# Layer norm of the last 1536 tokens in rows of features: normalization of already transposed x on VectorE in place of TensorE's transposition

## The chip, the cores and the metric

The kernel runs on one core of one Trainium2 chip. The metric is the device time of one execution in microseconds (us), the median of several runs; lower is better. The five engines of a core run their own queues of instructions, each in order, and meet only at semaphores: TensorE (PE in the profile; its weight loads are PEld), VectorE (DVE), ScalarE (ACT), GpSimd (POOL) and SyncE (SP), which here only issues DMAs.

## The reference

One transformer block on 2048 tokens of 512 features, all in float32: a layer norm without scale, 32-head attention with heads of 16 features, a gate computed by a two-layer perceptron with squared ReLU, and a residual.

```python
xn = _layernorm(x)                       # mean and variance over the 512 features
qkv = xn @ wqkv                          # 512 -> 3 * 512, split into q, k, v of 32 heads of 16
p = softmax(q @ k.T * 16 ** -0.5)        # 2048 x 2048 for each head
s = concat(p @ v) @ wo
h = relu(xn @ w1 + b1)                   # 512 -> 1792
g = silu((h * h) @ w2 + b2)              # 1792 -> 512
out = x + s * g
```

## The kernel before

A product of float32 matrices is made of three float32r products: each operand is split into a high part (`hi`) and the rest (`lo`), and the sum of hi·hi, hi·lo and lo·hi is accumulated in one bank of PSUM. With 512 features on 4 blocks of 128 partitions (`ko`), a tile of 128 x 512 outputs takes 12 matmuls.

The work has three stages. In the **opening** x is read, normalized, transposed and split into `xTs[c]` (features on partitions, 512 tokens of chunk c, hi and lo), and the first tiles of the projection are made: K, Q of the first 4 feature blocks (`qk_tile(4, c)` is the K tile and `qk_tile(0, c)` the Q tile of chunk c for heads 0 to 7) and V (`v_tile(c, tt)`, 128 tokens). In the **lead** (L1451 on) the other projection tiles run as half matmuls on both halves of TensorE's rows, between the first maxima of scores. In the **main loop** (L1675 on) scores, exponentials, the product with V, the perceptron and the output projection share TensorE.

The order of PE, ACT, DVE and POOL in the opening is written out by hand: each engine executes in the order in which the program emits instructions. SP's order in the opening is not by hand, it is set by the scheduler. The opening loop (L1327) goes over the 16 tiles of 128 tokens with a skew:

- `ln_stats(t)` (L1221): DVE takes the statistics of the tile (`bn_stats`, `bn_aggr`), ACT the square root.
- `ln_norm(t)` (L1229): DVE takes the reciprocal and the shift; for t of 2 and more ACT writes the normalized tile `xn` (L1241).
- `ln_high(t)` (L1244): PE transposes the tile by 4 matmuls with the identity (L1248) into a bank of PSUM, ACT copies it to the hi part (L1250). `ln_low(t)` (L1253): DVE subtracts for the lo part (L1256).
- `pump(n)` (L1264) emits n matmuls of the projection tiles: those of the list `ahead` first (`qk_first()`, that is the K and the Q tile of chunk 0 in halves of 256 tokens; then the K tiles of the later chunks), else those of `rest` (V and Q tiles).

A projection tile takes one of three PSUM banks (`se`, L1050) until `led` holds something. What is done with a finished tile stands in `qk_done` (L1072): with `quick`, ACT copies the hi part and DVE subtracts (`split_psum`, L104); else ACT copies it and POOL does both parts. While `hold[0]` is true, finished tiles wait for the next `let_go()`. Quick is for m of 0 and 4 after `hold[0]` is false, which before is after the loop. `v_done` (L1134) is one copy by ACT.

After the loop the rest of the opening follows: the K tiles left in `ahead`, the loads of the first K and Q heads (`load_k`, L1400, and `load_q`, L1402; both from DRAM, where K and Q were stored), the split of further weights, and the tiles of `rest` up to `v_tile(2, 0)` (L1407 to L1415). Then comes the lead, whose first score maximum needs the K of all 2048 tokens of the first head pair and Q of chunk 0.

`spill(c, k)` (L1308) stores the normalized x of a chunk to DRAM for the perceptron. Before, chunks 0 and 1 are spilled in the opening, 2 and 3 in the lead (`SPILLS`, rounds 5, 9, 13, 17).

Of the kernel before, what the change touches and what calls it, by code (L numbers as in the profile page):

```python
# [9 lines left out]
F32 = mybir.dt.float32  # L10
# [7 lines left out]
P = 128  # L18
S = 2048
D = 512  # L20
# [14 lines left out]
NXR = 16  # L35
EVAC = (1, 6, 7, 9, 11, 14)
# [3 lines left out]
SPILLS = (5, 9, 13, 17)  # L40
# [17 lines left out]
def kernel(  # L58
# [8 lines left out]
    b2: bass.AP,  # L67
    out: bass.AP,
# [12 lines left out]
    sp_d = dram.tile([S, D], F32, name="sp_d")  # L81
    xn_d = dram.tile([2, P, KO, S], F32, name="xn_d")
# [32 lines left out]
    with ExitStack() as ph:  # L115
# [42 lines left out]
        def load_k(qd, n):  # L158

            p, j, i = n // 6, n // 3 % 2, n % 3  # L160
            if n % 6 == 0:
                kas[qd, p] = ring("ka")
            h = 4 * qd + 2 * p + j
            nc.sync.dma_start(
                kas[qd, p][64 * j + DH * i : 64 * j + DH * (i + 1), :].bitcast(F32),
                k_d[h // 8][i % 2, (h % 8) * DH : (h % 8 + 1) * DH, :],
            )
# [850 lines left out]
        def qk_terms(m, c, ps):  # L1018
            wq, m0 = wq_cols(m)
            ms = slice(m0, m0 + P)  # L1020
            xT = xTs[c]
            t = terms3(ps, [
                (lambda a, q, ko=ko: wq[q, a, ko, ms], lambda b, q, ko=ko: xT[q, b, ko])
                for ko in range(KO)
            ])
            if m == 4 and c == 0:

                t = [t[k] for k in (0, 3, 6, 9, 2, 5, 1, 4, 7, 10, 8, 11)]
            return t
# [183 lines left out]
        def load_x(t):  # L1213
            xts[t] = xp.tile([P, D], F32, name="xt", bufs=12)
            nc.sync.dma_start(xts[t], xf[t * P : (t + 1) * P, :])

        mvs = {}
        rstds = {}
        pts_ = {}

        def ln_stats(t):  # L1221
            stats = xp.tile([P, 6], F32, name="stats")
            nc.vector.bn_stats(stats, xts[t])
            mvs[t] = xp.tile([P, 2], F32, name="mv", bufs=3)
# [3 lines left out]

        def ln_norm(t):  # L1229
            rstd = rstds.pop(t)  # L1230
            xn = xp.tile([P, D], F32, name="xn", bufs=3)
# [46 lines left out]
        def exp_mm(st, j, pts, spare):  # L1278
# [5 lines left out]
            else:  # L1284
# [10 lines left out]
                if all(t is not x for d in pts_all.values() for x in d.values())  # L1295
# [8 lines left out]
                    mybir.EngineType.Activation, mybir.EngineType.DVE, mybir.EngineType.Pool,  # L1304
                }
# [12 lines left out]
        raw_m = load_w("wm", 2 * P, ((0, P), (D, P)))  # L1318
        for t in range(2, 6):
            load_x(t)  # L1320
        raw_v = load_w("wv", D, ((2 * D, D),))
        for t in range(6, NT):
            load_x(t)
        for vt in vts:
            nc.vector.memset(vt[:, :, DH:], 1.0)
        fill_ring("ka", 0, -1.0)
        for i in range(NT + 3):  # L1327
            if i in (2, 3):

                kos = slice(2 * i - 4, 2 * i - 2)  # L1330
                if i == 2:
                    ln_norm(1)
                    ln_high(0)
                    split_w(wa_t, kos, slice(0, 2 * P), raw_m[:, kos])
                    ln_low(0)
                else:
                    ln_high(1)
                    split_w(wa_t, kos, slice(0, 2 * P), raw_m[:, kos])
                    ln_stats(2)
                    ln_low(1)  # L1340
                    ln_norm(2)
                    ln_stats(3)
            else:
                if i < NT:
                    ln_stats(i)
                if 0 <= i - 1 < NT:
                    ln_norm(i - 1)
                if 2 <= i - 3 < NT:
                    ln_low(i - 3)
                if i == 4:  # L1350

                    pump(10)
                if 0 <= i - 2 < NT:
                    ln_high(i - 2)
            if 5 <= i < 9:
                split_w(wa_t, i - 5, slice(2 * P, 2 * P + D), raw_v[:, i - 5], True)
            let_go()
            if 9 <= i < 11:
                fill_ring("ka", 1, -1.0, (32 + 64 * (i - 9),))
            if i in (11, 12):  # L1360
                fill_ring("qm", i - 11, 0.0)
            if i == 11:
                raw_r = [load_w("wv", 3 * P, ((P, 3 * P),))]
            if i in (13, 14):
                spill(0, i - 13)
            if i in (16, 18):
                spill(1, (i - 16) // 2)
            if i >= 4:
                pump({4: 6, 7: 14, 8: 12}.get(i, 8 if i < 7 else 7 if i < 11 else 6))
            if i == 3:  # L1370
                ahead.append(qk_first())
            if i >= 7 and (i - 3) % 4 == 3:
                c = (i - 3) // 4
                ahead.append(qk_tile(4, c))
                rest.append(qk_tile(0, c))
                order.append(("qk", 0, c))
            if i >= 3 and (i - 3) % 4 == 3:
                c = (i - 3) // 4
                rest += [v_tile(c, tt) for tt in range(4)]
                order += [("v", c, tt) for tt in range(4)]  # L1380
# [19 lines left out]
        for n in range(12):  # L1400
            load_k(0, n)
# [5 lines left out]
        pump(47)  # L1407
# [16 lines left out]
        lead.enter_context(tc.manual_schedule(engines={mybir.EngineType.SP}))  # L1424
# [10 lines left out]
        def lead_rounds():  # L1435
            for i in side_rounds(specs, single):
                if i % 6 == 0:
                    now[0] = i // 6
                    run_waiting()
                    if i // 6 in SPILLS:  # L1440
                        c, k = divmod(SPILLS.index(i // 6), 2)
                        spill(c + 2, k)
# [266 lines left out]
_INS = ['A_x', 'A_wqkv', 'A_wo', 'B_w1', 'B_b1', 'B_w2', 'B_b2']  # L1709
# [23 lines left out]
```

## Time and profile before

| what | value |
|---|---|
| time, median of 3 runs | 1621.21 us (1621.0 to 1621.35) |
| the profiled execution: time | 1621.38 us |
| the profiled execution: span of the core | 1619.6 us |
| TensorE busy | 1607.3 us, 99% of the span |
| VectorE busy | 1352.4 us, 84% |
| ScalarE busy | 1187.2 us, 73% |
| GpSimd busy | 534.1 us, 33% |

The profile is that of one execution, so its durations add up to that execution's own time of 1621.38 us, 1.8 us of which lie around the span. Busy shares are means over the whole span; the change touches the opening alone, which the views by window show.

### The profile page before, as it was taken

Reading aid. Unit: us, or ns where it says so; the run is one execution under the profiler, and the core shown is the slowest. Engines: PE = TensorE matmul, PEld = TensorE weight load, DVE = VectorE, ACT = ScalarE, POOL = GpSimd, SP = SyncE. Lnnn points to the kernel's source line nnn. Section 1 sums busy time; section 2 is a strip of 40 time slices with the busy share of each in tenths; the row PEclk is TensorE's granted clock in tenths of the full one; section 3 lists DMA queues with packets and bytes.
Section 4 is the critical chain, followed back from the end, with each engine's and each line's share of the span. In section 5 each row is a group of like instructions: output and inputs, shape, how many; then the busy total and the mean of one; then the engine's idle time right before and its main releaser. Section 6 shows DMA issues by size and latency. Waiting matters only on the chain.

```text
span 1619.6 us, 36065 instructions
## 1 busy us (share of the span) xinstructions
PE 1607.3 (99%) x13660; PEld 939.7 (58%) x13660; DVE 1352.4 (84%) x2307; ACT 1187.2 (73%) x2347; POOL 534.1 (33%) x610
## 2 busy tenths in 40 slices
PE   8999999999999999999999999999999999999998
PEld 7799665556545654664466446645654565445543
DVE  7486888888888888888888888888888888887754
ACT  7212777777777777877777777777777777778886
POOL 6436667133113311331133113311331123214621
PEclk9999999999999999999999999999999999999999
DMA  8967556434333333423333334323432252237655
GB/s 290 244 237 234 174 156 160 132 96 128 81 104 94 106 88 88 131 87 101 90 107 100 91 89 118 115 71 90 131 107 73 65 163 76 64 102 228 207 177 169
DMA packets 164173, 209.19 MB, mean 129 GB/s; under 512 B 59136, under 2 KB 79360, under 8 KB 162432
## 3 DMA queue, kind: packets, MB, share of 16 engines
q1 hardware_dynamic: 163856, 206.63, 43.9%
q8 instruction: 108, 1.77, 0.5%
q14 instruction: 65, 0.53, 0.1%
q10 hardware_dynamic: 144, 0.26, 0.0%
HBM read 148.90 MB, written 56.34 MB: 127 GB/s over the span
## 4 chain that ended last, share of the span: by engine, by line
PE 99%; DVE 1%; DMA 0%; issue 0%; ACT 0%; DVEq 0%
PE po L406 31%; PE pd_t L258 19%; PE pm_t L320 17%; PE se L1286 15%; PE pd_t L226 5%; PE pm_t L1157 4%; PE pm_t L226 1%; PE pd_t L1157 1%; PE se L1127 1%; PE se L1061 1%; PE se L320 1%; PE pm_t L1248 0%; PE pd_t L1127 0%; DVE mx L327 0%; PE po L1061 0%; DMA xt<-in_A_x_dram 0%
## 5 line engine op out<-in xcount | busy, mean ns | idle before, releaser
L327 DVE TENSOR_REDUCE mx<-pm_t 128x1 f32<-128x512 f32 x1910 | 1188.3, 684 | 174.5 <-PE pm_t L320 84.8
L1298 ACT ACTIVATE pt<-se 128x512 f32<-128x512 f32 x1894 | 975.4, 613 | 234.3 <-PE se L1286 187.0
L320 PE MATMUL pm_t<-ka,qm 64*128 64x512 f32 x1910 | 761.0, 419 | 0.0
L1286 PE MATMUL se<-qe,ka 64*128 64x512 f32 x2005 | 677.3, 396 | 0.0
L406 PE MATMUL po<-pt,v 128*32 128x512 f32 x3820 | 520.8, 605 | 0.2 <-DVE tsm L849 0.2
L320 PEld LDWEIGHTS pm_t<-ka,qm 64*128 64x128 f32 x1910 | 335.2, 184 | 236.0 <-DVE mx L327 224.5
L1286 PEld LDWEIGHTS se<-qe,ka 64*128 64x128 f32 x2005 | 338.9, 184 | 19.8 <-ACT xr L1298 1.7
L258 PEld LDWEIGHTS pd_t<-xc,w1s 64*128 64x128 f32 x2352 | 292.1, 187 | 82.2 <-issue 82.2
L258 PE MATMUL pd_t<-xc,w1s 64*128 64x256 f32 x2352 | 332.3, 288 | 0.0
L258 PE MATMUL pd_t<-w2t,hT 64*128 64x512 f32 x1080 | 300.1, 410 | 0.0
L258 PEld LDWEIGHTS pd_t<-w2t,hT 64*128 64x128 f32 x1080 | 179.3, 184 | 82.4 <-issue 75.5
L571 POOL TENSOR_TENSOR r<-r 128x512 f32<-128x512 f32 x56 | 58.2, 1040 | 353.5 <-ACT r L568 353.5
L406 PEld LDWEIGHTS po<-pt,v 128*32 128x32 f32 x3820 | 76.7, 108 | 147.1 <-issue 125.6
L327 DVE TENSOR_REDUCE mx<-se 128x1 f32<-128x512 f32 x121 | 77.9, 686 | 26.1 <-PE pm_t L1157 17.3
L590 POOL TENSOR_TENSOR u<-u,b_t 128x512 f32<-128x512 f32 x16 | 20.6, 1285 | 209.1 <-ACT u L589 209.1
L568 ACT ACTIVATE r<-pd_t,b_t 128x256 f32<-128x256 f32 x112 | 46.9, 470 | 57.1 <-PE pd_t L258 55.0
L99 POOL TENSOR_SCALAR sh<-tr 128x32 fp32r<-128x32 f32 x30 | 6.5, 217 | 213.6 <-DVE tr L371 213.6
L1157 PE MATMUL pm_t<-xT,wr_t 64*128 64x512 f32 x408 | 74.0, 388 | 0.0
L100 POOL TENSOR_TENSOR hT<-r,hT 128x512 fp32r<-128x512 f32 x56 | 72.2, 1290 | 4.7
L226 PE MATMUL pd_t<-w2t,hT 64*128 64x512 f32 x264 | 68.7, 392 | 0.0
L1157 PEld LDWEIGHTS pm_t<-xT,wr_t 64*128 64x128 f32 x408 | 60.7, 185 | 0.0
L455 POOL TENSOR_TENSOR ot<-ot,hl 128x512 f32<-128x512 f32 x27 | 34.7, 1285 | 65.4 <-DMA hl<-r_d 51.7
(177 smaller groups left out, 1398.9 us busy)
## 6 DMA issues: line engine op xcount, KB each, us to landing
w1s<-w_d SPq DMA_DIRECT2D x196, 256.0 KB
qm<-q_d SPq DMA_DIRECT2D x384, 32.0 KB
ka<-k_d SPq DMA_DIRECT2D x96, 128.0 KB
qe<-q_d SPq DMA_DIRECT2D x384, 32.0 KB
q_d<-hl SPq DMA_DIRECT2D x16, 512.0 KB
g<-g_d SPq DMA_DIRECT2D x32, 256.0 KB
k_d<-hl SPq DMA_DIRECT2D x15, 512.0 KB
on_d<-hl SPq DMA_DIRECT2D x116, 64.0 KB
```

The costliest lines, as they stand in the source:

```text
L100: (lo or nc.gpsimd).tensor_tensor(dst[1], raw, dst[0].bitcast(F32), op=ALU.subtract)
L226: mm = nc.tensor.matmul(out_, lh(r), rh(r), start=first_ and lane == 0, stop=last_ and lane == 1, skip_group_check=True,)
L258: mm = nc.tensor.matmul(out_, lh(r), rh(r), start=first_ and lane == 0, stop=last_ and lane == 1, skip_group_check=True,)
L320: nc.tensor.matmul(ps, qms[u][p][64 * j : 64 * j + 64, qb * P : (qb + 1) * P], kas[qd, p][64 * j : 64 * j + 64, kc * 512 : (kc + 1) * 512] ...
L327: return nc.vector.tensor_reduce(mxs[u][:, c, kc : kc + 1], ps, axis=AX.X, op=ALU.max)
L406: nc.tensor.matmul(po[32 * j : 32 * j + 32, :], vs[qd][:, (4 * kb + j) * VW : (4 * kb + j) * VW + 32], pts[j], start=(kb == 0), stop=(kb = ...
L455: nc.gpsimd.tensor_tensor(ot, ot, rb, op=ALU.mult)
L568: nc.scalar.activation(r[:, i], ps[:, i * CW : (i + 1) * CW], AF.Relu, bias=b1_t[:, fo : fo + 1])
L571: nc.gpsimd.tensor_tensor(r, r, r, op=ALU.mult)
L1157: mm = nc.tensor.matmul(out_, lh(r), rh(r), start=first_ and lane == first, stop=last_ and lane != first, skip_group_check=True,)
L1286: nc.tensor.matmul(se, kas[qd, j // 2][b : b + 64, kb * P : (kb + 1) * P], qes[u][j // 2][b : b + 64, :], start=True, stop=True,)
L1298: return nc.scalar.activation(pts[j], se, AF.Exp, scale=0.25)
```

## The change

The host hands over two more arrays: `x_t`, x with features in rows (for each chunk and each half of 256 tokens, 128 partitions by 4 blocks by 256 tokens), and `w_m`, the first K and Q weight columns in the layout of the tile that they are loaded to. Tokens 0 to 511 (chunk 0) are normalized and transposed as before. For chunks 1 to 3:

- the statistics of a tile still come from x with tokens in rows, and `bn_aggr` puts mean and variance into columns of a tile `lns[c]` of the chunk;
- `ln_rows(c)`: ACT takes the square root of the 4 variances at once, DVE the reciprocal and a transposition in blocks of 32, and SP writes 4 small pieces to DRAM as rows of 512 means and 512 factors;
- `ln_back(c)`: SP reads these rows back into all 128 partitions (512 KB);
- `ln_half(c, h)`: DVE subtracts the row of means from the half chunk and multiplies by the row of factors, two blocks at a time, in place; ACT copies the hi part, POOL subtracts for the lo part.

So the 48 transpositions of these tiles on TensorE, with their banks, the 12 hi copies by ACT from PSUM, the 12 lo subtractions by DVE and the 12 normalizations by ACT are gone. The loop of the opening is written out anew, with its pumps: the order of the matmuls after chunk 0 is now K of chunk 1, Q of chunk 1, K of chunk 2, K of chunk 3, V of chunk 1, Q of chunk 2, first V of chunk 2. `hold[0]` is false before the first K and Q tiles are done, so all of these are quick. The hi part of the V weights is made by ACT in place of POOL. `load_k` is issued in two parts of 1024 tokens. Chunk 1 is spilled in the lead, where `SPILLS` has two more rounds. SP's order is by hand in the opening as well. The buffers of x tiles go from 12 to 7, those of `xn` from 3 to 2.

```diff
-SPILLS = (5, 9, 13, 17)
+SPILLS = (5, 9, 13, 17, 21, 25)
...
+            elif m == 4:
+                t = [t[k] for k in (0, 3, 6, 9, 2, 5, 8, 11, 1, 4, 7, 10)]
...
         def ln_stats(t):
             stats = xp.tile([P, 6], F32, name="stats")
             nc.vector.bn_stats(stats, xts[t])
+            if t >= 4:
+                c, n = divmod(t, 4)
+                nc.vector.bn_aggr(lns[c][:, :8].rearrange("p (k t) -> p t k", k=2)[:, n], stats)
+                return
...
+        def ln_rows(c):
+            m = lns[c]
+            nc.scalar.activation(m[:, 4:8], m[:, 4:8], AF.Sqrt, bias=eps_t)
+            nc.vector.reciprocal(m[:, 4:8], m[:, 4:8])
+            tr = xp.tile([P, 32], F32, name="lnt")
+            nc.vector.transpose(tr, m)
+            for q in range(4):
+                nc.sync.dma_start(
+                    ln_d[c].rearrange("k t n -> (k t) n")[:, 32 * q : 32 * q + 32],
+                    tr[32 * q : 32 * q + 8],
+                )
+
+        def ln_back(c):
+            row = lnrs[c] = xp.tile([P, 2, 512], F32, name="lnr")
+            nc.sync.dma_start(
+                row.rearrange("p k n -> p (k n)"),
+                ln_d[c].rearrange("k t n -> (k t n)")[None, :].to_broadcast([P, 1024]),
+            )
+
+        def ln_half(c, h):
+            ns = slice(256 * h, 256 * h + 256)
+            row, raw, xT = lnrs[c], xrs.pop((c, h)), xTs[c]
+            pairs = (slice(0, 2), slice(2, 4))
+            for kos in pairs:
+                for k, op in ((0, ALU.subtract), (1, ALU.mult)):
+                    nc.vector.tensor_tensor(
+                        raw[:, kos], raw[:, kos], row[:, k : k + 1, ns].to_broadcast([P, 2, 256]), op=op
+                    )
+                nc.scalar.activation(xT[:, 0, kos, ns], raw[:, kos], AF.Copy)
+            for kos in pairs:
+                nc.gpsimd.tensor_tensor(
+                    xT[:, 1, kos, ns], raw[:, kos], xT[:, 0, kos, ns].bitcast(F32), op=ALU.subtract
+                )
+
+        def load_xt(c, h):
+            raw = xrs[c, h] = xp.tile([P, KO, 256], F32, name="xr_", bufs=3)
+            nc.sync.dma_start(raw, x_t[c, h])
...
+            else:
+                ln_low(3)
+                for ko in (2, 3):
+                    split_w(wa_t, ko, slice(2 * P, 2 * P + D), raw_v[:, ko])
+                for t in range(4, 8):
+                    ln_stats(t)
+                    if t == 4:
+                        load_x(11)
+                ln_rows(1)
+                ln_back(1)
+                for t in (12, 13, 14):
+                    load_x(t)
+                load_xt(2, 0)
+                ln_stats(8)
+                load_x(15)
+                hold[0] = False
+        def add_chunk(c):
+            if c:
+                ahead.append(qk_tile(4, c))
+                (ahead if c == 1 else rest).append(qk_tile(0, c))
+                order.append(("qk", 0, c))
+            rest.extend(v_tile(c, tt) for tt in range(4))
+            order.extend(("v", c, tt) for tt in range(4))
+        add_chunk(0)
+        ln_stats(9)
+        pump(24)
+        for t in (10, 11):
+            ln_stats(t)
+        ln_rows(2)
+        ln_back(2)
+        pump(12)
+        ln_half(1, 0)
+        load_xt(2, 1)
+        pump(6)
+        for t in (12, 13):
+            ln_stats(t)
+        ln_half(1, 1)
+        load_xt(3, 0)
...
+        pump(6)
+        for t in (14, 15):
+            ln_stats(t)
+        ln_rows(3)
+        ln_back(3)
+        pump(12)
+        ln_half(2, 0)
+        load_xt(3, 1)
+        pump(12)
+        add_chunk(1)
+        pump(6)
+        ln_half(2, 1)
...
+        pump(6)
+        ln_half(3, 0)
+        pump(12)
+        for n in range(12):
+            load_k(0, n, slice(0, 1024))
+        add_chunk(2)
+        ln_half(3, 1)
+        raw_r = [load_w("wv", 3 * P, ((P, 3 * P),))]
+        pump(12)
+        add_chunk(3)
+        pump(12)
+        for k in range(2):
+            spill(0, k)
...
         for n in range(12):
-            load_k(0, n)
+            load_k(0, n, slice(1024, S))
         qms[0] = load_q(0, "qm")
...
-        pump(47)
```

More of the change, by code (lines that the diff above doesn't have):

```diff
@@ L35 @@
 NXR = 16
+NXT = 7
 EVAC = (1, 6, 7, 9, 11, 14)
@@ L1218 @@
         rstds = {}
+        lnrs = {}
+        xrs = {}
+        lns = {c: xp.tile([P, 32], F32, name=f"lns{c}", bufs=1) for c in range(1, 4)}
+        for m in lns.values():
+            nc.vector.memset(m, 1.0)
         pts_ = {}
```

125 lines of the change are left out of this document (63 added, 62 removed).

## The prediction, made before the changed kernel ran

> **What bounds the kernel now.** I read the page's first part, then the busy times by window of the first 60 us, then the chain of work that ended last in that stretch, then DVE's, POOL's and SP's timelines beside it.
>
> ```profile
> PE 1607.3 (99%) x13660; PEld 939.7 (58%) x13660; DVE 1352.4 (84%) x2307; ACT 1187.2 (73%) x2347; POOL 534.1 (33%) x610
> ```
>
> TensorE is the bound of the whole, so a microsecond by which the opening is longer or shorter should stand in the total. The change is confined to the opening.
>
> ```profile
> core 0: us, PE busy (x) PEld busy (x) DVE busy (x) ACT busy (x) POOL busy (x), PEclk, DMA share, GB/s
> 0.00:10.00 10.00, 2.92 (x12) 2.41 (x13) 5.82 (x25) 4.29 (x8) 5.68 (x10) 1.00 0.82 275
> 10.00:20.00 10.00, 10.00 (x68) 9.96 (x68) 9.33 (x30) 8.57 (x17) 8.16 (x9) 1.00 0.82 303
> 20.00:30.00 10.00, 10.00 (x54) 8.23 (x53) 8.09 (x26) 8.71 (x19) 8.31 (x8) 1.00 0.68 196
> 50.00:60.00 10.00, 10.00 (x45) 8.04 (x44) 0.00 (x0) 1.80 (x3) 7.33 (x10) 1.00 0.83 116
> ```
>
> PE is full from 10 us on. DVE is nearly as full as PE until 30 us (9.33, then 8.09 of 10) and has nothing to do at 50 to 60. So the question is not what PE saves, but whether DVE, which receives the work, can deliver in time.
>
> ```profile
> 9.02 2.60 PE se L1061 x10
> ...
> 15.72 0.44 PE pm_t L1248 x4
> ...
> 17.55 1.67 PE se L1061 x14
> ...
> 19.89 2.32 PE se L1127 x10
> ...
> 37.32 0.44 PE pm_t L1248 x4
> 37.75 2.79 PE se L1127 x12
> ...
> 60.13 2.80 PE pd_t L1127 x12
> ```
>
> The chain is PE without a gap. From 15.72 to 37.32 it holds 12 groups of 4 transpositions at 0.44 us: tiles 4 to 15, those that the change removes. A projection tile is 12 matmuls in 2.80 us (0.233 each). The last one ends at 60.13 + 2.80 = 62.93: there the lead begins. I work out this moment for the changed kernel.
>
> **What is removed.** On PE, 12 x 0.44 = 5.3 us, all on the path. On ACT 12 normalizations and 12 copies, on DVE 12 subtractions and 12 pairs of small operations, all hidden before. With PE alone the lead would begin at 57.6.
>
> **What is added, DVE first.** Its in-order queue goes on from `ln_low(3)`:
>
> ```profile
> 15.39 0.68 DVE L1256 TENSOR_TENSOR xT<-pm_t,xT 128x512 fp32r<-128x512 f32 x1
> 15.98 0.68 DVE L1223 BATCH_NORM_STATS2 stats<-xt 128x6 f32<-128x512 f32 x1
> 16.70 0.18 DVE L1225 BATCH_NORM_AGGREGATE mv<-stats 128x2 f32<-128x6 f32 x1
> 16.80 0.13 DVE L1232 RECIPROCAL rstd<-rstd 128x1 f32<-128x1 f32 x1
> ```
>
> From start to start a 128x512 operation takes about 0.60 us (15.39 to 15.98) if the next does not need it, else its full 0.68; statistics of one tile take 0.72 + 0.10 = 0.82. After the change `ln_low(3)` still waits for PE and ACT; I put its end at 15.5, up to 0.5 earlier than before since fewer statistics stand ahead of it.
>
> ```profile
> L371 DVE STREAM_TRANSPOSE tr<-m 128x32 f32<-128x32 f32 x32 | 6.5, 202 | 0.1
> L1227 ACT ACTIVATE rstd<-mv,eps_t 128x1 f32<-128x1 f32 x16 | 4.7, 294 | 4.0 <-DVE mv L1225 2.4 <-DVE rstd L1232 1.4
> L106 DVE TENSOR_TENSOR hl<-se,hl 128x512 fp32r<-128x512 f32 x2 | 1.4, 692 | 7.0 <-ACT hl L105 7.0
> L100 POOL TENSOR_TENSOR hl<-raw,hl 128x512 fp32r<-128x512 f32 x5 | 6.5, 1292 | 0.4
> L815 DVE TENSOR_TENSOR g<-g,s 128x512 f32<-128x512 f32 x12 | 8.8, 741 | 0.3
> L380 SPq DMA_DIRECT2D sh_d<-sh x32: 319/320/432, 118.9 to 1554.3; - x32
> L441 SPq DMA_DIRECT2D hl<-r_d x27: 540/552/594, 240.2 to 1419.6; - x27
> 0.74 2.75 DMA xt<-in_A_x_dram
> ```
>
> 1. Statistics of tiles 4 to 7: 4 x 0.82 = 3.3, to 18.9. Square root 0.29, reciprocal 0.15, transposition 0.20, with hand-overs: 19.7.
> 2. The rows go through DRAM. Four small writes, issued at 0.34 each by SP, the last at 20.8. A write's landing is not in the trace; the first x tile took 2.75 from issue, of which its 256 KB at the 380 GB/s of full queues are 0.7, so I take 2.1 to 2.2 for a small one: 23.0. The broadcast of 512 KB (issue 0.55, then 3.0) lands at 26.6. SP waits there, and the loads of x tiles 12 to 15 behind it land by about 30, before they are needed.
> 3. Meanwhile DVE does the statistics of 8 to 11 (3.3), the quick subtractions of the first K and Q tiles (1.3) and the second chunk's rows (0.8): free at 25.1. The rows are the later: `ln_half(1, 0)` begins at 26.6. Landings of 1.0 less each would give 25.1; of 4.1 (K's last store, before, 47.48 to 51.61) about 30.
> 4. The six halves are 24 operations of 128x512 with both operands in SBUF. Their nearest row is L815 (two SBUF operands; least 0.65). That one operand is a broadcast row has no price in the trace at 512; I take none. With a mean of 0.62 for dependent and independent ones, 14.9 us.
>
> **The price that I think decides** is that these 24 meet POOL's 12 subtractions of 1.29 us, which read SBUF at the same time.
>
> ```profile
> 1564.13 0.69 DVE L813 TENSOR_TENSOR g<-pd_t,g 128x512 f32<-128x512 f32 x1 [0.33 <-PE pm_t L1286]
> 1564.38 0.73 POOL L100 TENSOR_TENSOR hl<-ot,hl 128x256 fp32r<-128x256 f32 x1
> 1583.99 1.82 DVE L815 TENSOR_TENSOR g<-g,s 128x512 f32<-128x512 f32 x2
> 1584.07 1.20 POOL L100 TENSOR_TENSOR hl<-tot,hl 128x256 fp32r<-128x256 f32 x1
> ```
>
> At 1564 DVE reads one operand from PSUM: POOL's subtraction takes its plain 0.73. At 1584 DVE has two operations with both operands in SBUF, and everything stretches: POOL's takes 1.20 instead of 0.73, the two of DVE 1.82 instead of some 1.25. 1.25 + 0.73 is 1.98, near the whole stretch of 1583.99 to 1585.81: they ran one after the other. The Trainium skill (SBUF — State Buffer, section Who interferes with whom) says that a VectorE instruction with two SBUF inputs and a GpSimd instruction that reads SBUF exclude each other for their whole length. The trace agrees with it.
>
> So from 26.6 on one port carries the 24 operations (14.9) and, ahead of the last of them, 10 of the 12 subtractions (12.9): 54.4. Statistics of tiles 12 to 15 and two quick subtractions lie beside POOL's. Moments in which neither uses the port (the third chunk's square root; the quick subtraction that stands behind ACT's copies) I put at 1.4: DVE ends `ln_half(3, 1)` at 55.8.
>
> **PE.** The first K and Q tiles end at 19.89 less three transposition groups: 18.6. Four V tiles take 11.2, and 0.7 is lost since the second needs the bank of the first K tile, which DVE frees at about 22.0: chunk 0 is used up at 30.5. Then K of chunk 1 needs both halves of chunk 1, by the same working at 34.6, and the bank of a V tile whose copy stands on ACT behind the hi copies: 35.8. K of chunk 3, in this order only two tiles after Q of chunk 1, is the last to wait: 55.8, 0.65 for ACT's copy, 10 matmuls of 0.233, 0.3 for the last lo part: 59.1. Six tiles follow without a wait: 59.1 + 6 x 2.80 = 75.9. That is 13.0 us later than 62.93.
>
> **Two smaller prices.** PE is idle for 5 to 7 us twice. At the start, after its first idle time, 10 matmuls of 256 columns took 2.60 us (0.26 each), later 14 took 1.67 (0.12), while the granted clock reads 1.00. From 9.02 to 15.72 the chain holds 24 of them in 5.0 us. At 0.12 they would be 2.9. So a restart may cost 0 to 2.1, with the transpositions between them up to 3.0. The Trainium skill (TensorE: Matmul & The Clock Gate, Part 1: The HAM clock gate) halves the clock after an idle window of some 3.4 us for about as long; by it the last restart would cost an estimated 1.7.
>
> SP's queue now runs in the written order: it holds the second halves of the K loads and then Q until K of chunk 3 is stored, and all of them behind the bias loads.
>
> ```profile
> 25.18 3.59 SPq L1397 DMA_DIRECT2D b_t<-in_B_b_dram  x1
> ...
> 47.48 0.38 SPq L1016 DMA_DIRECT2D k_d<-hl  x1
> ...
> 51.61 6.42 SPq L164 DMA_DIRECT2D ka<-k_d  x12
> 58.80 4.61 SPq L153 DMA_DIRECT2D qm<-q_d  x5
> ```
>
> K of chunk 3 is ready to be stored at 61, lands at about 64; biases (up to 4) keep SP until 64 to 68; 12 loads take 6.4 and six of Q 3.0 and a landing of 2: Q is there at 76 to 79.5. Against 75.9 that is 0 to 3.5. The two overlap: a PE that restarts slowly waits less for Q. I take 2.0 for both together. The extra 4.5 MB (rows of x_t and broadcasts) ride in the DMA queues beside the wait for DVE. The spill of chunk 1 moves into the lead, where I cost it at nothing; it would matter if it held back K or Q loads, which come earlier in the same queue.
>
> **Sum.** 13.0 + 2.0 = 15.0 on 1621.4 of the profiled execution: 1636.4; its median stands 0.2 lower: **1636.2**.
>
> **Rivals.**
> - *DVE alone sets the pace, port free* (0.18). If POOL and DVE can run beside each other here, DVE's own queue is left: 26.6 + 14.9 + statistics 3.3 + rows 0.8 + quick subtractions 1.2 + waits for ACT and for dependent results 4.1 = 50.9. Lead at 70.8: +7.9, 1629.2, up to 1631 with a slow restart. For it: only one place of the trace shows the collision at 512 elements. Against: that place is clean.
> - *No change* (0.09). If also the waits vanish (rows land early, ACT never late), DVE has 15.5 + 12 x 0.82 + 3 x 0.35 + 24 x 0.60 + 4 x 0.60 = 43.2, the lead begins at about 63, and the time is 1621 to 1624.5. This is the floor of my own prices, which is why I hold a gain to be unlikely.
> - *PE keeps the pace, faster* (0.05). The one mechanism: the halves are ready before PE asks, at 30.5, 36 and 39, and the 5.3 us are kept: 1616. It decides at the end of `ln_half(3, 1)`: under 39.9 the gain exceeds 3.2 us. From the floor of 43.2 that asks for less than 0.47 per operation of 512 elements; no DVE row with two operands of that size is under 0.65.
> - *K and Q loads still later* (0.06): landings of 4 us in each of the round trips, two of them in line, add 4 and more to the forecast: 1641 to 1647.
>
> **Chances and range.** Forecast 0.62, with a range of its own of 1632 to 1642. The range of 8 in 10 reaches down over the free port and up over some of the late loads: 1627 to 1643. A measurement of this kernel can tell about 0.2%, 3.2 us, from no change. Faster by more 0.05, within 0.09, slower 0.86.
>
> **What would show it.** In the windows of the changed kernel PE's count falls from 45 per 10 us to under 30 between 30 and 57, and DVE is busy at 40 to 55, where it was idle. The chain should run over the subtract and multiply of `ln_half` and the first lead matmul start at 73 to 80. If port sharing is right, the group of these operations has a mean near 0.9 us and POOL's subtraction shows over 1.4; if wrong, 0.7 and 1.29, with the lead at 71. If chunk 1's broadcast lands after 28, step 2 is short. I am wrong altogether if PE stays full from 10 to 60 us.

## The result, and the profile after

| | before | changed |
|---|---|---|
| time, median | 1621.11 us (1620.78 to 1621.35, 4 runs) | 1644.69 us (1644.6 to 1646.86, 4 runs) |
| profiled execution: time | 1621.38 us | 1644.64 us |
| profiled execution: span | 1619.6 us | 1642.8 us |

The ratio is 1.0149, with a 95% interval of 1.0131 to 1.0166: slower by 1.5%, clear of noise. The forecast was 1636.2 us with a range of 1627 to 1643. The direction was right; the time lies 1.7 us above the range. Between the profiled executions the loss is 1644.64 - 1621.38 = 23.3 us, where the forecast had 15.0.

The first line is the busy time of each engine over the whole span, and the fence below it the windows of 10 us from 30 to 90 us:

```profile
PE 1611.2 (98%) x13612; PEld 929.0 (57%) x13612; DVE 1364.9 (83%) x2308; ACT 1179.5 (72%) x2330; POOL 543.0 (33%) x610
```

```profile
core 0: us, PE busy (x) PEld busy (x) DVE busy (x) ACT busy (x) POOL busy (x), PEclk, DMA share, GB/s
30.00:40.00 10.00, 5.40 (x17) 3.98 (x16) 5.88 (x13) 2.55 (x5) 7.89 (x6) 0.83 0.66 215
40.00:50.00 10.00, 5.59 (x17) 3.70 (x16) 8.62 (x10) 3.50 (x6) 6.54 (x6) 0.76 0.74 241
50.00:60.00 10.00, 5.64 (x14) 3.74 (x13) 6.72 (x10) 3.49 (x6) 7.51 (x8) 0.67 0.59 209
60.00:70.00 10.00, 10.00 (x40) 8.10 (x39) 0.69 (x1) 3.33 (x7) 2.40 (x3) 0.89 0.79 269
70.00:80.00 10.00, 10.00 (x45) 7.64 (x44) 0.69 (x1) 2.46 (x5) 9.53 (x14) 1.00 0.83 224
80.00:90.00 10.00, 4.67 (x23) 3.52 (x22) 3.10 (x5) 1.43 (x2) 0.82 (x1) 0.66 0.46 159
```

In the kernel before, the two windows that the prediction doesn't show are these:

```profile
30.00:40.00 10.00, 10.00 (x55) 8.32 (x54) 5.81 (x15) 7.15 (x14) 4.54 (x8) 1.00 1.03 382
40.00:50.00 10.00, 10.00 (x45) 8.04 (x44) 1.38 (x2) 4.04 (x8) 6.37 (x8) 1.00 0.98 336
```

So TensorE executed 45 to 55 matmuls in each 10 us between 30 and 60 us and was full. Now it executes 17, 17 and 14 there. There is a second hole, which the forecast had only as 0 to 3.5 us: 23 matmuls between 80 and 90 (before, 88, of the lead), when the projection tiles are done. The granted clock (PEclk) falls with the holes, to 0.83, 0.76, 0.67 and again 0.66; before, it read 1.00 in every window up to 100 us.

TensorE's timeline says what each hole waits for. Its columns are start, duration, engine, line, operation, tile, shape, count, and in brackets the idle time ahead of the group and what ended it:

```profile
35.23 7.27 PE L1067 MATMUL se<-xT,wa_t 128*128 128x512 f32 x24 [4.60 <-ACT vt L1142]
46.80 5.69 PE L1067 MATMUL se<-xT,wa_t 128*128 128x512 f32 x12 [4.30 <-ACT xT L1272]
56.74 5.82 PE L1067 MATMUL se<-xT,wa_t 128*128 128x512 f32 x12 [4.25 <-ACT xT L1272]
62.40 2.94 PE L1133 MATMUL se<-wa_t,xT 128*128 128x512 f32 x12
...
79.22 0.50 PE L1163 MATMUL pm_t<-wa_t,xT 64*128 64x512 f32 x1
...
85.52 0.76 PE L324 MATMUL se<-ka,qm 64*128 64x512 f32 x1 [5.33 <-DMA qm<-q_d]
```

The three K tiles (chunks 1, 2, 3) each wait over 4 us: the first for a bank that ACT frees by a copy that stands behind its hi copies, the others for the hi copies themselves, and these wait for DVE. The last one is done at 62.40, six tiles follow without a wait, and the lead begins at 79.22. The first matmul of the maxima (L324) then waits 5.33 us for Q, until 85.52. Before, these two moments were:

```profile
62.86 0.50 PE L1157 MATMUL pm_t<-wa_t,xT 64*128 64x512 f32 x1
...
63.44 0.39 PE L320 MATMUL se<-ka,qm 64*128 64x512 f32 x1
```

So of the 23.3 us, 79.22 - 62.86 = 16.4 arise until the lead begins and (85.52 - 79.22) - (63.44 - 62.86) = 5.7 from there to the first maxima. The remaining 1.2 follow at once: the rows of the maxima from 85.52 on take 0.62 to 0.79 us where they took 0.39 before. From the first rows of the maxima on the two traces run alike.

DVE's timeline is where the first 16.4 come from:

```profile
26.30 2.75 DVE L1269 TENSOR_TENSOR xr__237<-xr__237,lnr 128x512 f32<-128x512 f32 x4 [1.35 <-DMA lnr<-ln_d]
...
30.58 3.46 DVE L1269 TENSOR_TENSOR xr__239<-xr__239,lnr 128x512 f32<-128x512 f32 x4
...
39.99 2.75 DVE L1269 TENSOR_TENSOR xr__394<-xr__394,lnr 128x512 f32<-128x512 f32 x4 [3.55 <-DMA lnr<-ln_d]
42.66 4.76 DVE L1269 TENSOR_TENSOR xr__475<-xr__475,lnr 128x512 f32<-128x512 f32 x4
48.60 0.69 DVE L110 TENSOR_TENSOR hl<-se,hl 128x512 fp32r<-128x512 f32 x1 [1.18 <-ACT hl L109]
49.35 3.04 DVE L1269 TENSOR_TENSOR xr__498<-xr__498,lnr 128x512 f32<-128x512 f32 x4
53.57 0.69 DVE L110 TENSOR_TENSOR hl<-se,hl 128x512 fp32r<-128x512 f32 x1 [1.18 <-ACT hl L109]
54.18 3.17 DVE L1269 TENSOR_TENSOR xr__549<-xr__549,lnr 128x512 f32<-128x512 f32 x4
```

The six groups of four are the six halves of `ln_half`, and the last ends at 54.18 + 3.17 = 57.35. Two kinds of loss stand in them. The groups take 2.75 us where nothing disturbs them (0.69 an operation) and 3.46, 4.76, 3.04 and 3.17 where POOL subtracts beside them: together 19.93 instead of 6 x 2.75 = 16.50, so 3.4 us of contention. And DVE stands still: 3.55 us for the broadcast rows of chunk 2, twice 1.18 for ACT's copy of a quick split.

In the chain of work that ended last (start, duration, link) the rows of statistics are these:

```profile
20.86 1.18 DMA ln_d<-lnt
22.19 4.01 DMA lnr<-ln_d
...
29.01 6.79 DMA ln_d<-lnt
35.81 4.16 DMA lnr<-ln_d
39.99 0.71 DVE xr__394 L1269
```

The first two links are the rows of chunk 1, the next two those of chunk 2. The broadcasts take about the same (4.01, 4.16); the small write takes 1.18 for the one and 6.79 for the other. SP's queue shows what stood ahead of each, and what stood ahead of Q in the second hole:

```profile
23.06 1.82 SPq L1221 DMA_DIRECT2D xt<-in_A_x_dram  x2
24.92 0.43 SPq L1280 DMA_DIRECT2D xr__394<-in_A_x_t_dram  x1
...
26.99 2.58 SPq L1251 DMA_DIRECT2D ln_d<-lnt  x4
...
64.41 1.51 SPq L1364 DMA_DIRECT2D xn_d<-xT  x2
66.03 2.14 SPq L1496 DMA_DIRECT2D ka<-xT  x2
68.21 1.61 SPq L1500 DMA_DIRECT2D b_t<-in_B_b_dram  x1
69.87 4.71 SPq L1503 DMA_DIRECT2D b_t<-in_B_b_dram  x1
74.68 6.54 SPq L168 DMA_DIRECT2D ka<-k_d  x12
81.26 5.52 SPq L157 DMA_DIRECT2D qm<-q_d  x12
```

The second row writes are issued behind loads of x and x_t and the stores of the first K and Q tiles. And from 64.41 to 74.58 SP is occupied by two spills, two copies into `ka` and the two bias loads, before it comes to the second K loads and, behind those, to Q. By 62.40 the matmuls of the last K tile were done, so those 10 us of SP seem to stand in the path of the first maxima; the first experiment tests it.

### The profile page after: what moved, and what is told of

Its sections match the earlier page's. It is cut to its first block, busy times and chain, and to the rows that moved or that the text cites. A ratio compares the mean times of both kernels' runs of the same rounds, so it can differ in the third digit from the quotient of the medians.

```text
span 1642.8 us, 35979 instructions
## 1 busy us (share of the span) xinstructions
PE 1611.2 (98%) x13612; PEld 929.0 (57%) x13612; DVE 1364.9 (83%) x2308; ACT 1179.5 (72%) x2330; POOL 543.0 (33%) x610
## 4 chain that ended last, share of the span: by engine, by line
PE 95%; DVE 2%; SPq 1%; DMA 1%; issue 1%; ACT 0%; DVEq 0%; ACTq 0%
PE po L410 31%; PE pd_t L262 19%; PE pm_t L324 17%; PE se L1339 14%; PE pd_t L230 5%; PE pm_t L1163 4%; PE pm_t L230 1%; PE pd_t L1163 1%; PE se L324 1%; DMA lnr<-ln_d 0%; DMA ln_d<-lnt 0%; SPq L168 0%; DVE xr__475 L1269 0%; SPq L1503 0%; PE po L1163 0%
## 5 line engine op out<-in xcount | busy, mean ns | idle before, releaser
L324 PE MATMUL pm_t<-ka,qm 64*128 64x512 f32 x1910 | 760.8, 419 | 0.0
L324 PEld LDWEIGHTS pm_t<-ka,qm 64*128 64x128 f32 x1910 | 335.2, 184 | 236.1 <-DVE mx L331 224.7
L1163 PEld LDWEIGHTS pm_t<-xT,wr_t 64*128 64x128 f32 x408 | 57.0, 185 | 6.5
```

Of the source, the lines that this page charges most:

```text
L324: nc.tensor.matmul(ps, qms[u][p][64 * j : 64 * j + 64, qb * P : (qb + 1) * P], kas[qd, p][64 * j : 64 * j + 64, kc * 512 : (kc + 1) * 512] ...
L1163: mm = nc.tensor.matmul(out_, lh(r), rh(r), start=first_ and lane == first, stop=last_ and lane != first, skip_group_check=True,)
```

## The experiments

The theory after the result, A in most of the texts below: four losses in one chain, namely rows that land late, DVE's 24 operations beside POOL, a slow TensorE clock after each hole, and SP's order at the start of the lead. Each experiment takes one away. Each was measured beside the kernel before on the same chip, which read 1621.0 to 1621.3 us every time; the changed kernel's 1644.69 us is the base of the differences.

### The order of SP's queue

```diff
-        for k in range(2):
-            spill(0, k)
...
+        for n in range(12):
+            load_k(0, n, slice(1024, S))
+        qms[0] = load_q(0, "qm")
+        for k in range(2):
+            spill(0, k)
```

The second K loads and Q go ahead of the spills, the copies into `ka` and the biases; nothing else moves.

> The two spills of chunk 0, the two copies of chunk 0 and both bias loads go behind the second K loads and the Q loads in SP's queue; nothing else changes. Theory A (SP's written order holds back Q): in the changed kernel Q's first loads land at 85.5 us while TensorE has been ready since 79.2. Without the 10 us of issues in between, K of chunk 3 lands at about 66.5 to 68, twelve loads of 0.46 and six of Q give 76.5 to 78, so the wait of 5.3 us and the slow restart behind it go: first maxima matmul at about 79.7, time 1637.5 to 1639.5. Theory B (Q is held by the landing of K of chunk 3 or by full DMA queues, not by the order): no change, 1644 to 1645.

Measured: 1639.78 us (1639.35 to 1640.73), ratio 1.0116 (1.0101 to 1.0131): 4.9 us less than the changed kernel. TensorE's timeline of this kernel at the first maxima:

```profile
79.74 0.49 PE L324 MATMUL se<-ka,qm 64*128 64x512 f32 x1 [0.29 <-DMA qm<-q_d]
```

The wait for Q is 0.29 instead of 5.33, and the matmul itself takes 0.49 instead of 0.76, since TensorE did not stand still before it. That settles the second hole: it was the order of SP's queue. It was worth more than the total says. The first maxima start 5.8 us earlier (79.74 for 85.52) and the slow rows behind them, 1.2 us, are gone too, yet the time falls by 4.9 only. About 2 us are lost again later in the lead, where TensorE waits for ACT, and ACT for a load of weights that SP now issues behind what was moved back:

```profile
100.42 1.76 ACT L999 ACTIVATE wr_t<-wv 128x384 fp32r<-128x384 f32 x4 [7.12 <-DMA wv<-in_A_wqkv_dram]
102.72 0.50 PE L1163 MATMUL pd_t<-wa_t,xT 64*128 64x512 f32 x1 [1.69 <-ACT vt L1142]
```

### POOL's use of the port

```diff
-                nc.gpsimd.tensor_tensor(
-                    xT[:, 1, kos, ns], raw[:, kos], xT[:, 0, kos, ns].bitcast(F32), op=ALU.subtract
-                )
+                nc.gpsimd.memset(xT[:, 1, kos, ns].bitcast(F32), 0.0)
```

> The lo parts of chunks 1 to 3 are left out: GpSimd writes zeros there and reads nothing. Theory A (the port that VectorE's operations with two SBUF operands share with GpSimd's reads costs VectorE time): every group of four subtract and multiply operations takes 2.75 us, as the first did, in place of 2.75, 3.46, 2.75, 4.76, 3.04 and 3.17; behind the rows of chunk 2, which the DMA sets, 2.7 us are gained, and the same at K of chunk 3 and at the end: 1641.5 to 1642.5. Theory B (the port costs nothing that counts): 1644 to 1645, with groups as long as before.

Measured: 1643.74 us (1642.93 to 1644.69), 1.0 less, between the two expectations; the intervals overlap (1.0125 to 1.0155 against 1.0131 to 1.0166), so the 1.0 is not sure. DVE's timeline of this kernel, the fourth and fifth halves:

```profile
41.95 2.74 DVE L1269 TENSOR_TENSOR xr__475<-xr__475,lnr 128x512 f32<-128x512 f32 x4
...
48.67 2.74 DVE L1269 TENSOR_TENSOR xr__498<-xr__498,lnr 128x512 f32<-128x512 f32 x4 [2.12 <-DMA lnr<-ln_d]
```

All six groups now take 2.71 to 2.75. POOL's reads are what stretched them, by 3.4 us in all. The Trainium skill (SBUF — State Buffer, section Who interferes with whom) describes the pair of ports as an exclusive lock, and this agrees with it: the fourth half took 4.76 us beside POOL's subtractions and takes 2.74 without. But the time falls by less than a third of the 3.4: DVE is ready for the fifth half at 46.55 instead of 49.35 and then waits 2.12 us for the rows of chunk 3. Most of the contention was covered by the late rows.

### The way of the rows through DRAM

```diff
-                ln_d[c].rearrange("k t n -> (k t n)")[None, :].to_broadcast([P, 1024]),
+                xf[2 * c : 2 * c + 2].rearrange("t d -> (t d)")[None, :].to_broadcast([P, 1024]),
```

> The broadcast of a chunk's rows reads 4 KB of x in place of the means and factors, so it waits for nothing; the rows are still made and written. What is normalized is not the reference's. Theory A (the round trip of the rows through DRAM is on the path): the halves of chunk 1 begin at 25 in place of 26.3, those of chunk 2 at about 36.5 in place of 40.0, K of chunk 3 and everything behind it 2.5 to 3.5 us earlier: 1641 to 1642.5. Theory B (VectorE's own queue sets the end, the wait is taken back by less contention later): at most 1 us, 1643.5 to 1645.

Measured: 1640.46 us (1639.91 to 1641.32), 4.2 less. In DVE's timeline the first half of chunk 2 starts without a wait worth the name:

```profile
35.47 2.75 DVE L1269 TENSOR_TENSOR xr__394<-xr__394,lnr 128x512 f32<-128x512 f32 x4 [0.30 <-DMA lnr<-in_A_x_dram]
```

That is 4.5 us before the changed kernel's 39.99, and K of chunk 3 starts 4.5 earlier too (52.24 for 56.74). The whole of it reaches the end, but for 0.3: somewhat more than theory A expected.

### TensorE's clock

```diff
+            for n in range({4: {2: 10, 3: 18}}.get(m, {}).get(c, 0)):
+                nc.tensor.matmul(
+                    ps, wa_t[:, 0, 0, 0:P], xTs[0][:, 0, 0, :], start=True, stop=True
+                )
```

Matmuls that nobody reads fill part of the waits ahead of K of chunks 2 and 3.

> 10 and 18 extra matmuls on chunk 0 ahead of K of chunk 2 and K of chunk 3, whose results are overwritten; they run while TensorE is idle. Theory A (the idle time lowers TensorE's clock, granted 0.67 at 50 to 60 us): K of chunk 3, twelve matmuls in 4.5 to 5.7 us now, takes 2.8 to 3.3, all behind it moves 1.5 to 2.2 us earlier: 1642.3 to 1643.2, and the granted clock of 30 to 60 us is 0.9 or more. Theory B (those matmuls wait for their operands): no change or some later, 1644.5 to 1646.

Measured: 1643.56 us (1641.72 to 1644.39), 1.1 less. The windows of this kernel:

```profile
40.00:50.00 10.00, 8.28 (x34) 5.83 (x33) 8.26 (x10) 3.50 (x6) 7.08 (x6) 1.00 0.75 233
50.00:60.00 10.00, 7.45 (x32) 5.44 (x31) 6.61 (x10) 3.50 (x6) 7.42 (x8) 1.00 0.61 217
```

The granted clock stays at 1.00, where it was 0.76 and 0.67. With it the last ten matmuls of K of chunk 3 take 2.60 us, and V begins at 60.39 instead of 62.40. K starts only 0.1 us earlier (56.63 for 56.74), so the slow clock cost 1.9 of these 2.0 us at this place. Little of that reaches the end: Q still comes when SP's queue lets it, and the clock falls to 0.66 in that wait as before. The interval of the runs is wide here (1.0118 to 1.0151 against 1.0131 to 1.0166), so the 1.1 is not sure, and the time lies between the two expectations. The 2.0 in the trace is what this run shows.

### Both orders: SP's queue and TensorE's tiles

```diff
+        pump(24)
...
+        qms[0] = load_q(0, "qm")
+        for n in range(12):
+            load_k(0, n, slice(1024, S))
+        for k in range(2):
+            spill(0, k)
```

Q's loads go ahead of the second K loads, and two V tiles of chunk 1 go ahead of K of chunk 3, to fill TensorE's last wait with work that has to be done anyway.

> On top of the queue of e1: Q loads ahead of the second K loads, and on TensorE K of chunk 2 and two V tiles of chunk 1 ahead of the last half chunk's work, then K of chunk 3, then the rest. No work is taken away. Theory A (most of the loss is that TensorE stands idle for K of chunk 3 with ready V tiles behind it in its order, and that Q waits in SP's order): TensorE idles at 30 to 36 and little after, K of chunk 3 ends at about 61, the lead's first maxima matmul comes at 72 to 75 in place of 85.5 and 79.7, time 1630 to 1634. Theory B (VectorE and the round trip of K of chunk 3 set the lead's start whatever the order): as e1, 1639 to 1641.

Measured: 1637.09 us (1636.07 to 1638.41), 7.6 less than the changed kernel and 2.7 less than with SP's order alone. That lies between the two expectations. K of chunk 3 starts at 57.83 without a wait, and the lead begins some 5 us earlier (73.81), but then the maxima wait for K. SP's queue of this kernel:

```profile
63.70 10.00 SPq L157 DMA_DIRECT2D qm<-q_d  x12
73.75 5.66 SPq L168 DMA_DIRECT2D ka<-k_d  x12
```

Twelve loads of Q took 10.00 us here, 5.51 with SP's order alone, where they stood behind K's; what holds them is not told by this run. K's loads behind them are then the late ones: the first matmul of the maxima starts at 74.39, a later one waits 2.96 us for `ka` until 78.65.

### The queue that writes the rows

```diff
-                nc.sync.dma_start(
+                nc.scalar.dma_start(
```

> The four small writes of each chunk's rows are issued by ScalarE, in a queue of their own, in place of SyncE; the broadcast stays with SyncE. Theory A (the writes of chunk 2 take 6.8 us since they stand behind 2.8 MB of loads and stores in the same queue): they land in 2 to 3 us, the broadcast is issued at about 28, the halves of chunk 2 begin at 36 to 37 in place of 40, the time is 2 to 3.5 us under the changed kernel: 1641 to 1643. Theory B (the 16 engines are full, whichever queue a write comes from, or a round trip through DRAM is that long): halves at 39 to 40, 1644 to 1645.

Measured: 1643.72 us (1642.76 to 1644.78), 1.0 less, again between the two expectations and not clear of noise (ratio 1.0138, 1.0123 to 1.0153). The chain of this kernel, for the same rows of chunk 2:

```profile
26.66 3.96 DMA ln_d<-lnt
30.69 6.43 DMA lnr<-ln_d
37.14 0.70 DVE xr__394 L1269
```

The write lands in 3.96 instead of 6.79 and is issued earlier, so the broadcast goes out 5.1 us earlier (30.69 for 35.81). But the broadcast stays in SP's queue, and there it takes 6.43 instead of 4.16: it seems that a part of the waiting only moved to it. The normalization starts 2.9 us earlier. The next half then takes 5.78 instead of 4.76 for its four operations, where POOL subtracts beside them from 40.37 to 45.03 without a pause, and the lead still waits for Q (5.62). The Trainium skill (DMA: Bandwidth & Descriptors, section Queues, rings and completion order) says that each DMA engine consumes the descriptors of a ring in order and that SP and ACT have a ring each on every DMA engine; the landing of 3.96 us by ACT's queue, for 6.79 by SP's, agrees with that.

### SP's order by the scheduler

The list of engines in the written order lacks SP again in the opening, as it did before the change; from the lead on SP's order is by hand in all of these kernels.

```diff
-                    mybir.EngineType.SP,
```

> SyncE's order in the opening is left to the scheduler as in the kernel before, all else as changed. It puts one spill and the small bias load earlier, but the two copies, the large bias load and the second spill stay ahead of the second K loads. Theory A (the length of what stands between K of chunk 3 and Q counts): Q about 2 to 3 us earlier, 1641.5 to 1643. Theory B (it does not): 1644 to 1645.

Measured: 1641.81 us (1640.5 to 1642.28), 2.9 less. That is the time of theory A, but not by its reason alone: Q's loads are issued 3.7 us earlier (77.56 for 81.26), while the first hole grows. The scheduler's order brings chunk 1's and chunk 3's rows later (the fifth half starts at 52.15, after a wait of 3.44 us for `lnr`) and the lead begins later, at 82.24 instead of 79.22; yet the maxima start at 82.81 without a wait for Q. It mends the second hole and makes the first one worse. Neither order is good.

### Both orders and ACT's queue together

> e5 and e6 together. Theory A (the waits for order and for rows are in series): 2 to 3 us under e5. Theory B (behind the order of e5 VectorE has slack, so that rows that come earlier change nothing): as e5 to 0.7 us.

Measured: 1635.12 us (1633.43 to 1635.79), ratio 1.0084 (1.0067 to 1.0101). With the other orders in place ACT's queue for the rows is worth 2.0 us (1637.09 to 1635.12), where alone it was worth 1.0. So orders and queues account for 9.6 of the 23.6 us between the medians.

### Half of DVE's operations

```diff
-                for k, op in ((0, ALU.subtract), (1, ALU.mult)):
+                for k, op in ((0, ALU.subtract),):
```

On the kernel of the last experiment.

> e8 with the multiplication by the factors left out: 12 of the 24 operations of VectorE with two operands in SBUF are gone, some 8 us, all else stands. Theory A (behind rows and order, VectorE's work on the halves is what TensorE still waits for): K of chunk 3 and the lead 3 to 6 us earlier than in e8, 1629 to 1632.5. Theory B (the rows' way through DRAM and the loads of K and Q are the rest): within 1.5 us of e8, 1633.5 to 1636.

Measured: 1630.28 us (1629.78 to 1631.18), 4.8 less than with the multiplication. Twelve operations at 0.69 are 8.3 us of DVE; 4.8 of them come through to the end; a part of the rest goes into the wait for the rows of chunk 2, which is 2.93 us here and was 0.52 with the multiplication. DVE's operations are a large part of what is left when the orders are mended, and half of them gone is still slower than before (ratio 1.0055, 1.004 to 1.0071). The 9.3 us that remain in this run are not taken apart any further.

### Only the last chunk

The kernel before, with chunk 3 alone in rows of features, its rows written by ACT's queue, and K of chunk 3 behind Q and the first V tile of chunk 1.

```diff
-                if i < NT:
+                if i < 12:
...
+        pump(24)
+        for h in range(2):
+            ln_half(h)
+        pump(24)
+        ahead.append(qk_tile(4, 3))
```

> The kernel before, with only the last chunk (tokens 1536 to 2047) in rows of features: 16 of the 64 transpositions of TensorE go (1.8 us), the statistics of these four tiles, the rows (written by ScalarE's queue) and two halves go to VectorE after its work for chunk 2, and K of chunk 3 stands behind Q and the first V tile of chunk 1, so that TensorE has work until the halves are ready; chunk 1 is spilled in the lead. Theory A (what the changed kernel loses, it loses since three chunks are asked of VectorE one behind the other with TensorE waiting; one chunk, late, has room): TensorE stays full, the lead's first maxima matmul comes at 61.5 to 63.5 (63.4 before), time 1619.3 to 1621.2. Theory B (the form itself costs more than the transpositions wherever it stands): K of chunk 3 comes after 47, the lead at 65 or later, 1623 or more.

Measured: 1628.38 us (1627.23 to 1629.16, 5 runs), ratio 1.0045 (1.0032 to 1.0057). DVE's and TensorE's timelines of this kernel:

```profile
42.66 7.42 DVE L1262 TENSOR_TENSOR xr<-xr,lnr 128x512 f32<-128x512 f32 x8 [4.04 <-DMA lnr<-ln_d]
```

```profile
49.47 0.80 PE L1063 MATMUL se<-xT,wa_t 128*128 128x512 f32 x1 [5.62 <-ACT xT L1265]
51.26 5.06 PE L1063 MATMUL se<-xT,wa_t 128*128 128x512 f32 x11 [1.00 <-POOL xT L1267]
```

TensorE has no wait until 43.8 (49.47 less 5.62), so the first ten tiles cost nothing. But the way through DRAM is now the last thing: DVE waits 4.04 us for the rows, then needs 7.42 for eight operations, and TensorE waits 5.62 + 1.00 us and restarts slowly (eleven matmuls in 5.06 us). The rows are late although ACT's queue writes them: DVE has them ready at 31.62, the four issues keep ACT's queue from 32.78 to 36.70, the broadcast goes out at 38.38, and DVE begins at 42.66. What holds these issues is not told by this run, and no run makes the rows earlier.

### Only the last chunk, and its K later

```diff
-        pump(24)
+        pump(48)
         ahead.append(qk_tile(4, 3))
...
-        while ahead:
-            pump(1)
+        pump(12)
```

> The kernel of h1_last (that before, with only chunk 3 in rows of features and its rows written by the ACT queue), with K of chunk 3 placed three V tiles later on TensorE: behind Q and the V tiles 0 to 2 of chunk 1, and ahead of the last V tiles. In h1_last TensorE waited 5.62 us for K of chunk 3 while V tiles that were ready stood behind it. Theory A: that order was all that h1_last lost. Then TensorE has no such wait (under 1 us), K of chunk 3 lies at about 49.5 to 53.5, the first matmul of the maxima starts at 62 to 64.5 (before: 63.44), and the time is 1620 to 1622.5. Theory B: the K that comes later is stored and loaded again later, and the first maxima wait for it or for Q instead: the first matmul of the maxima may start as early, but waits of over 2 us stand behind it in the maxima, and the time is 1624 or more. Either way no gain over the kernel before is expected beyond 1 us, since TensorE only saves twelve transpositions of about 0.44 us at most, and DVE gets the eight two-operand operations instead of copies.

Measured: 1633.77 us (1632.87 to 1634.61, 5 runs), ratio 1.0077 (1.0064 to 1.0091): slower than the run before by 5.4. Theory B holds. TensorE's timeline:

```profile
51.51 4.38 PE L1129 MATMUL se<-wa_t,xT 128*128 128x512 f32 x12 [4.85 <-ACT vt L1138]
55.73 2.94 PE L1063 MATMUL se<-xT,wa_t 128*128 128x512 f32 x12
...
75.02 0.79 PE L322 MATMUL se<-ka,qm 64*128 64x512 f32 x1 [7.10 <-DMA ka<-k_d]
```

(The transpositions saved are 16, four groups of 0.44 us, not the twelve that the expectation names.) The work moved ahead does not fill the hole: its third V tile needs a bank that ACT frees, and ACT, which works in order, stands in the hi copies of `ln_half` until DVE delivers. K of chunk 3 then starts 6.3 us later than in the run before (55.73 for 49.47). The lead begins earlier, at 66.96 instead of 70.78, but K, stored and loaded again, arrives only at 75.02. One order leaves TensorE waiting for the normalization, the other for K's way through DRAM. Of the two the earlier K costs less. No version that I tried beats the kernel before. That none could is not shown: a version with chunk 3 alone whose rows are ready sooner was not tried.

## Why the direction was right and the size too small

Point by point, in the order of its steps:

- **What is removed**: right. TensorE has 48 matmuls fewer (13660 to 13612), and the saving shows nowhere, since TensorE waits.
- **Rows of chunk 1**: right. Forecast 26.6, measured 26.30; the first wait of TensorE was forecast until 35.8 and ended at 35.23. Two errors nearly cancel in the 26.6: the write landed in 1.18 us, not 2.2, and the broadcast took 4.01, not 3.6.
- **Rows of chunks 2 and 3**: not priced. The forecast took 2.1 to 2.2 for a small write and applied it to the first chunk only. For chunk 2 the write took 6.79; ahead of it in SP's queue stood loads of x and x_t, which the forecast had put at nothing. By ACT's queue it took 3.96, so the queue is a part of the cause; what made up the rest is open. DVE waited 3.55. Taking the round trip away gained 4.2 us on the total, the largest single item but for SP's order.
- **The port, the price thought to decide**: the mechanism is there, but this step failed by its weight. The signs named for it came (the 24 operations have a mean of 0.83 us, POOL's subtractions of 1.50). But the forecast had 12.9 us of POOL's subtractions in series with DVE's operations, and the overlap cost DVE 3.4 us and the end about 1.0, which is not clear of noise: most of POOL's work fell beside DVE's statistics and beside its waits, when it held nothing up. That the last half still ended at 57.35, near the forecast 55.8, is luck. From 26.30 on, 31.05 us are made up of 16.5 for 24 operations (0.69 each, not 0.62: 1.6 more than forecast), 3.4 of contention (9.5 less), 6.3 of waiting (3.55, twice 1.18 and 0.37 for a square root; 4.9 more than the 1.4 forecast) and, by difference, 4.8 of statistics and quick subtractions, which the forecast had laid beside POOL's work at nothing.
- **K of chunk 3**: short by 1.8. The forecast let its 10 last matmuls run at 0.233 each and end at 59.1, 3.3 us behind the last half. K ended 5.05 us behind it (62.40), its last ten matmuls at about 0.43 each: TensorE had just been idle for 4.25 us. The filler showed that this is the clock: 1.9 us. Slow restarts had been named, but only the last one was priced, inside the joint 2.0.
- **Six tiles**: right, 62.40 + 6 x 2.80 = 79.2.
- **The joint 2.0 for SP's queue and the restart**: this is the step that failed and carried the time out of the range. It measured 5.7 + 1.2 = 6.9. The forecast let SP come to the second K loads at 64 to 68 and put 11.4 from there to Q (6.4, 3.0 and a landing of 2). SP came to them at 74.68, and 10.8 later the maxima began: the second part was right, the first was not. Ahead of those loads stood 1.51 of spills, 2.14 of copies into `ka` and 1.61 + 4.71 of biases, where the forecast had only the biases, "up to 4". The spills are those of chunk 0, which the changed program writes there; the prediction thought of the spill of chunk 1 alone, in the lead, and put it at nothing. The run with SP's order shows what they cost. There SP, with nothing else to issue, comes to the second K loads at 68.78, 5.6 us after it issued K's last store (63.19), where the forecast had 3 for that landing. So about half of the 10 us would have passed in waiting for K in any case; the other half held Q back, and it is the 5.0 us by which the wait for Q fell (5.33 to 0.29).

The sum: 15.0 forecast, plus 16.4 - 13.0 = 3.4 until the lead (1.6 in DVE's end, 1.8 in the clock), plus 6.9 - 2.0 = 4.9 behind it, is 23.3, as measured. The rival with late K and Q loads gave 1641 to 1647, where the time fell, with a chance of 0.06. That is in the main luck. K's landing was late, as it says (5.6 us in the run with SP's order), but with that landing alone the maxima waited 0.29 us; what stands in SP's queue was not in it.

The rival with a free port was settled by the run without POOL's subtractions: without them the time falls by about 1.0 us, not by the 7 between that rival and the forecast. (By that rival's own terms its lead begins at 50.9 + 3.3 + 16.8 = 71.0, not 70.8.) So neither the serial port nor the free one gives the time: the rows' way through DRAM (4.2 us) and SP's order (4.9) each cost more. What stays open is why Q's twelve loads took 10.00 us in one order and 5.51 in another, and why a bias load kept SP for 4.71 us.

## What to carry to other kernels

When a step moves work to a new engine, write out the queue of everything that moves with it, in order, up to the first instruction that the end waits for: here the DMAs that came ahead of Q cost more than the contention on which most of the thinking went. A round trip of a few kilobytes through DRAM is not cheap because it is small: price it with what stands ahead of it in the queue. Another queue for the writes gained 2.0 us once the orders were mended, and not clearly anything before; another queue for the broadcast was not tried. Moving entries back is not free either, since a load that something later waits for may stand behind them. And a saving on the full engine (5.3 us of TensorE here) is worth nothing once that engine waits for its replacement, the less so as the granted clock fell to 0.67 in such a wait here.

## What the hardware showed beyond that

- The granted clock follows TensorE's idle time within one stage: 0.83, 0.76, 0.67 in the windows with waits of 4.25 to 4.60 us, then 0.89 and 1.00 in the two windows that are full again. A matmul of 512 columns took about 0.43 us instead of 0.233 in the 3.2 to 5.7 us after such a wait.
- The same small DRAM write landed in 1.18 us for chunk 1 and in 6.79 for chunk 2, with loads of x and x_t ahead of it in SP's queue. Sent by ACT's queue the second one took 3.96, and then the broadcast took 6.43 instead of 4.16.
- Two-operand operations of DVE beside POOL's subtractions: a group of four took 2.75 us alone and up to 5.78.
- The same bias load (the second of the two) kept SP for 4.71 us ahead of the second K loads and for 2.20 behind them, in the kernel with SP's order alone.
